# Another order of the attention part's steps in an explicit instruction sequence

## The chip, the cores and the metric

The kernel runs on one core of a Trainium2 chip. The metric is the device time of one execution in microseconds (us); three runs of the kernel before gave a median of 977.19 us (974.65 to 978.02). The engines are named as in the profile: PE (matrix products), DVE (vector), ACT (scalar functions), POOL (the second elementwise engine) and SP, which here only issues transfers.

## The reference

Three layers follow one another: sparse attention, and two feed-forward layers with different gates. 4 batches of 8 heads, 576 rows, 64 columns per head; the attention's output is 2304 rows of 512.

```python
scores = scale * np.matmul(q, k.transpose(0, 1, 3, 2))
thresh = np.max(scores, axis=-1, keepdims=True) - tau
scores = np.where(scores >= thresh, scores, -1000000000.0)
attn = np.exp(scores - np.max(scores, axis=-1, keepdims=True))
attn = attn / (np.sum(attn, axis=-1, keepdims=True) + 1e-09)
x = np.matmul(attn, v)                # then (B, H, S, D) -> (B*S, H*D)
h = x @ w_in                          # 512 -> 2048
g = h * np.tanh(np.log1p(np.exp(h)))
y = g @ w_out                         # 2048 -> 512
h = y @ w_in2
out = (h * np.clip(h + 3.0, 0.0, 6.0) / 6.0) @ w_out2
```

## The kernel before, in words

**Numbers.** Products of the feed-forward layers are made from pairs of f16 parts (a high part and a low rest) with three matmuls for each product. The weights come as 64-bit words and are converted on the chip, in eight groups for each matrix: `lr` loads a group of 1 MB (line 759), `zw` takes its maximum on DVE (line 681), `zd`, `zp`, `zt`, `zf` make a scale from it (ACT, PE, DVE, DVE), `c0_g_` scales on ACT (line 800), `c0_g_0` and `c0_g_1` shift on POOL (line 807), `c0_g_l` joins in the low words on DVE (line 820), `h` writes the high part on ACT (line 840), and `u` the low part on POOL (through line 627). Two buffers hold raw groups; group g+2 can be loaded when `c0_g_l` is done with group g.

**Attention.** Pairs of heads (n = 0 to 15, four to a batch) are worked through in query tiles c = 0 to 3 of 128 rows and a last one, c = 4, that holds 64 rows of both heads. The steps of a tile, for heads j = 0 and 1: `s` scores on PE (line 1697), `pk` the peak on DVE (line 1706), `ex` the exponential on ACT (line 1716), `th` the threshold on ACT (line 1711), `mk` the mask on DVE (line 1719), `ph` the high part on ACT (line 1724), `pl` the low part on POOL (line 627), `tr` a transpose done by a transfer on SP (line 1732), `pv` the product with v on PE (line 1745). Then `dt`, `dr`, `dn` normalise two tiles on DVE, `fl` transposes them on PE, and `xh` and `xl` write the two parts of x. There are two banks for scores (one head in each), so a score waits for the mask of the tile before; four buffers each for exponentials and for f16 parts; three for transposed tiles (`PV_DEEP`). The values of a batch need `lv` loads, `vm` maxima on DVE (line 1592), a common scale (`ve`, `zdv`, `zpv`, `ztv`, `vq`), and `vh` and `vl`, the two parts. `lk`, `lq` load k and q, `kh` scales k on ACT, `qp` pads q on POOL.

**First layer.** When all four pairs of a batch have x for 256 rows (a block), `g{fp}{j}_{i}_0_{blk}` are its products with `w_in` on PE (line 1112): 96 steps of two matmuls to a block, feature groups fp = 0 to 7 in order, each wanting its weight group. `t` takes the result out, `hs` stores it to memory, and it is read again for the gate when the attention is over. Of the nine blocks six are worked on during the attention in steps of two matmuls; PE does them between the steps of attention.

**Order.** Nothing is chosen at run time. `SEQUENCE` (line 62) lists all 4098 steps as name@engine, and `Plan.run` (line 565) issues them in that order. Each engine executes its own steps strictly in this order, SP its transfers too; between engines only data and buffers make one wait for another. A buffer goes to the next step that asks for it in the sequence, from those given back before, so the order also settles which buffer a step has to wait for.

Of the kernel before, what the change touches and what calls it, by code (L numbers as in the profile page):

```python
# [67 lines left out]
s1_0_0@pe vh1@act vl0@dve ph0_1_0@act s1_0_1@pe vl1@dve ph0_1_1@act pk1_0_0@dve vh2@act pl0_1_0@pool pk1_0_1@dve
ex1_0_0@act zw0_0@dve th1_0_0@act ex1_0_1@act kh0_3@act mk1_0_0@dve vh3@act mk1_0_1@dve s1_1_0@pe tr0_1_0@sp
ph1_0_0@act vl2@dve zd0_0@act s1_1_1@pe ph1_0_1@act pk1_1_0@dve pl1_0_0@pool pv0_0_0@pe pk1_1_1@dve ex1_1_0@act  # L70
zw0_1@dve th1_1_0@act ex1_1_1@act lv0_1@sp lv1_1@sp zp0_0@pe mk1_1_0@dve lv2_1@sp tr1_0_0@sp mk1_1_1@dve ph1_1_0@act
s2_0_0@pe zt0_0@dve ph1_1_1@act zf0_0@dve s2_0_1@pe zd0_1@act pl1_1_0@pool pk2_0_0@dve c0_0_@act pv0_1_0@pe
pk2_0_1@dve ex2_0_0@act vm1_1@dve th2_0_0@act zp0_1@pe ex2_0_1@act c0_0_1@pool mk2_0_0@dve tr1_1_0@sp mk2_0_1@dve
c0_0_0@pool ph2_0_0@act s2_1_0@pe zt0_1@dve ph2_0_1@act dt0_0@dve s2_1_1@pe dr0_0@dve pl2_0_0@pool zf0_1@dve dn0_0@dve
zx0_0_0@act pk2_1_0@dve c0_1_@act fl0_0@pe pk2_1_1@dve pv1_0_0@pe ex2_1_0@act tr2_0_0@sp c0_1_1@pool vm2_1@dve
th2_1_0@act ex2_1_1@act mk2_1_0@dve c0_1_0@pool pv1_1_0@pe xh0_0@act mk2_1_1@dve ph2_1_0@act c0_0_l@dve ph2_1_1@act
s3_0_0@pe s3_0_1@pe lr0_2@sp h0_0_@act xl0_0@dve u0_0_1@pool pk3_0_0@dve dt1_0@dve u0_0_0@pool ex3_0_0@act pk3_0_1@dve
dr1_0@dve th3_0_0@act vm0_1@dve ex3_0_1@act pl2_1_0@pool mk3_0_0@dve mk3_0_1@dve ph3_0_0@act s3_1_0@pe zw0_2@dve
ph3_0_1@act s3_1_1@pe tr2_1_0@sp pl3_0_0@pool dn1_0@dve pk3_1_0@dve fl1_0@pe zd0_2@act pv2_0_0@pe pk3_1_1@dve
ex3_1_0@act th3_1_0@act c0_1_l@dve ex3_1_1@act tr3_0_0@sp xh1_0@act mk3_1_0@dve h0_1_@act mk3_1_1@dve s0_2_0@pe  # L80
ph3_1_0@act u0_1_1@pool xl1_0@dve ph3_1_1@act s0_2_1@pe vl3@dve lr0_3@sp zp0_2@pe pk0_2_0@dve u0_1_0@pool lv3_1@sp
pv2_1_0@pe zt0_2@dve ex0_2_0@act pk0_2_1@dve pl3_1_0@pool zf0_2@dve th0_2_0@act ex0_2_1@act mk0_2_0@dve c0_2_@act
# [15 lines left out]
pk2_2_1@dve pv1_2_0@pe xh0_4@act xs0_4@sp pl1_4_0@pool th2_2_0@act zpv1_1@pe g11_6_0_0@pe zw0_5@dve ex2_2_1@act
tr1_3_0@sp g11_8_0_0@pe g11_10_0_0@pe g20_0_0_0@pe t1_0_0@act g20_2_0_0@pe qp5@pool g20_4_0_0@pe g20_6_0_0@pe
kh0_5@act g20_8_0_0@pe g20_10_0_0@pe g21_0_0_0@pe g21_2_0_0@pe g21_4_0_0@pe g21_6_0_0@pe c0_4_l@dve zd0_5@act  # L100
g21_8_0_0@pe g21_10_0_0@pe g30_0_0_0@pe tr1_4_0@sp t2_0_0@act g30_2_0_0@pe g30_4_0_0@pe mk2_2_1@dve g30_6_0_0@pe
h0_4_@act g30_8_0_0@pe g30_10_0_0@pe g31_0_0_0@pe mk2_2_0@dve s2_3_0@pe ph2_2_1@act u0_4_0@pool ztv1_1@dve lr0_6@sp
# [1916 lines left out]
```

## Time and profile before

| | |
|---|---|
| median of three runs | 977.19 us (974.65 to 978.02) |
| profiled execution | 974.99 us, span of its instructions 973.2 us |
| PE busy | 923.1 us, 95% of the span |
| DVE busy | 767.7 us, 79% |
| ACT busy | 649.9 us, 67% |
| POOL busy | 401.6 us, 41% |
| granted PE clock, mean | 0.975 |
| transfers | 164.47 MB, 169 GB/s over the span |

The profile's second part cuts the span into 40 slices: PE stands at 3, 6, 7, 9, 6 and 8 tenths in the first six and at 9 (90% or more) from there to the next to last slice; the DMA engines stand at 9 or 8 in the first 18 slices and fall behind them. The attention ends near 400 us. A row of a timeline gives start and duration of an instruction, engine, line, operation, what it writes and reads, and in brackets how long its engine had stood idle and what ended that. The waits are sums by engine and line over a stretch.

### The profile page before, as it was taken

The numbers are of one execution on the slowest core, as the hardware profiler recorded it, in microseconds if no ns is written. First come the engines' busy times: TensorE is split into PE (matmuls) and PEld (weight loads), VectorE is DVE, ScalarE is ACT, GpSimd is POOL, SyncE is SP. The second block draws the span as 40 slices with busy tenths as digits, with TensorE's granted clock in tenths as the row PEclk, the third lists the DMA queues.
The fourth block names the chain that finished last, engine by engine and source line by source line (L and its number), as shares of the span: only waits on it lengthen the run. The fifth ranks groups of instructions, "written<-read, shape, count | busy, mean of one in ns | idle before, by whom it ended". The sixth has DMA issues, their size and how long they took to land.

```text
span 973.2 us, 25802 instructions
## 1 busy us (share of the span) xinstructions
PE 923.1 (95%) x10776; PEld 798.0 (82%) x10776; DVE 767.7 (79%) x1432; ACT 649.9 (67%) x1051; POOL 401.6 (41%) x354
## 2 busy tenths in 40 slices
...
GB/s 320 192 240 225 245 220 216 243 252 204 252 227 260 230 215 242 232 242 177 232 229 177 287 178 303 246 212 20 61 27 37 61 24 39 62 23 40 24 1 45
DMA packets 201798, 164.47 MB, mean 169 GB/s; under 512 B 174161, under 2 KB 174929, under 8 KB 195281
## 3 DMA queue, kind: packets, MB, share of 16 engines
...
q10 hardware_dynamic: 240, 0.20, 0.1%
...
HBM read 84.28 MB, written 36.04 MB: 124 GB/s over the span
## 4 chain that ended last, share of the span: by engine, by line
PE 84%; DVE 7%; POOL 3%; DMA 3%; issue 2%; ACT 1%; SPq 0%; DVEq 0%; POOLq 0%; ACTq 0%
PE h_g L1112 17%; PE y_y L1226 17%; PE s_s L1697 8%; PE aux_pv L1745 6%; PE hp_g1a L1299 5%; PE h_g0a L1299 5%; PE hp_g1d L1299 2%; PE h_g0d L1299 2%; POOL p_ph L627 2%; PE h_g1b L1299 1%; PE hp_g0b L1299 1%; DMA pt_tr<-p_ph 1%; PE y_y___1_6_0_13898 L1449 1%; PE y_y___1_0_0_10254 L1449 1%; PE y_y___1_4_0_12684 L1449 1%
## 5 line engine op out<-in xcount | busy, mean ns | idle before, releaser
L627 POOL TENSOR_TENSOR p_ph<-e_ex,p_ph 128x128 f16<-128x128 f32 (+3 forms) x160 | 185.8, 1184 | 110.6 <-issue 54.9
L1449 PEld LDWEIGHTS <-gs_oh 128*128 128x128 f16 x1512 | 146.8, 98 | 16.6
L1299 PEld LDWEIGHTS <-w__h 128*128 128x128 f16 x2016 | 156.0, 98 | 0.6
L1706 DVE TENSOR_REDUCE nm_pk<-s_s 128x1 f32<-128x576 f32 x144 | 104.7, 751 | 31.1 <-PE s_s L1697 30.0
L1719 DVE SCALAR_TENSOR_TENSOR e_ex<-s_s,thr_th,e_ex 128x576 f32<-128x576 f32 x144 | 111.8, 811 | 18.2 <-ACT thr_th L1711 13.6
L1716 ACT ACTIVATE e_ex<-s_s,nm_pk 128x576 f32<-128x576 f32 x144 | 104.2, 730 | 17.8 <-DVE nm_pk L1706 14.8
L1697 PE MATMUL s_s<-kd_lk,qs_qp 64*128 64x288 f32 x440 | 80.7, 481 | 35.7 <-DVE e_ex L1719 26.8
L1724 ACT ACTIVATE p_ph<-e_ex 128x576 f16<-128x576 f32 x144 | 94.7, 679 | 11.5 <-DVE e_ex L1719 8.8
L1299 PEld LDWEIGHTS <-w__u 128*128 128x128 f16 x1008 | 98.6, 98 | 0.0
L1745 PEld LDWEIGHTS <-pt_tr 128*128 128x128 f16 x2016 | 81.6, 103 | 10.8 <-issue 6.9
L1697 PEld LDWEIGHTS s_s<-kd_lk,qs_qp 64*128 64x128 f32 x440 | 41.3, 204 | 56.9 <-issue 39.8
L1745 PE MATMUL aux_pv<-vh,pt_tr 128*128 128x65 f16 (+1 forms) x1296 | 86.8, 203 | 1.0 <-DMA pt_tr<-p_ph 1.0
L627 DVE TENSOR_TENSOR gs_oh<-g_ab,gs_oh 128x896 f16<-128x896 f32 x72 | 74.6, 1086 | 14.9 <-ACT gs_oh L1399 14.9
L1399 ACT ACTIVATE gs_oh<-g_ab 128x1792 f16<-128x1792 f32 x36 | 59.6, 1690 | 27.2 <-DVE g_ab L627 27.2
L1745 PE MATMUL aux_pv<-vl_vl,pt_tr 128*128 128x64 f16 x720 | 71.0, 203 | 0.0
L1383 ACT ACTIVATE g_ab<-g_ab,aux,hscales 128x512 f32<-128x512 f32 x72 | 54.1, 805 | 17.1 <-DVE g_ab L1327 17.1
L1160 ACT ACTIVATE he_t<-h_g,hin 128x512 f32<-128x512 f32 x63 | 42.9, 683 | 23.0 <-PE h_g L1112 19.0
L1197 ACT ACTIVATE hp_e<-hl_l 128x512 f32<-128x512 f32 x72 | 42.5, 596 | 21.7 <-DVE gs_gh L1206 21.3
L1389 DVE SCALAR_TENSOR_TENSOR g_ab<-g_ab,f 128x512 f32<-128x512 f32 x72 | 51.2, 746 | 5.0 <-ACT g_ab L1383 5.0
L1206 DVE SCALAR_TENSOR_TENSOR gs_gh<-hp_e,fscales,gs_gh 128x512 f16<-128x512 f32 x72 | 52.9, 742 | 2.1 <-ACT gs_gh L1200 2.0
L1200 ACT ACTIVATE gs_gh<-hp_e,fscales 128x512 f16<-128x512 f32 x72 | 47.4, 680 | 9.4 <-PE y_y L1226 8.8
L1317 ACT ACTIVATE s_ka<-h_g0a 128x512 f32<-128x512 f32 x27 | 16.1, 595 | 48.3 <-PE h_g0a L1299 48.2
...
## 6 DMA issues: line engine op xcount, KB each, us to landing
...
```

The source lines that it names most:

```text
L627: engine[e].tensor_tensor(dst, a, b, ALU.subtract)
L1112: mm(hv[:, j, :], wj[:, wl, c * P : (c + 1) * P], x.tile[:, c, xl, :], start=j == 0 and n == 0, stop=j == 1 and n == 11, skip_group_check= ...
L1226: mm(yv[:, h, :], wt[1][f // 2].tile[:, f % 2, wl, c * P : (c + 1) * P], gs[fp // COL].tile[:, fp % COL, gl, f % 2, :], start=fp == 0 and ...
L1299: mm(dst.tile[:, i * Q : (i + 1) * Q], wt[2][fp][wl].tile[:, right - 1, c * P : (c + 1) * P], x[xl].tile[:, c, left - 1], start=first and ...
L1399: nc.scalar.activation(part.tile[:, :, 0], g.tile[:, :, 1:], AF.Copy)
L1449: mm(region(p), part[:, gl, left - 1], wt[3][fp][wl].tile[:, right - 1], start=fp == n == 0 and spot(p)[1] == 0, stop=fp == NG - 1 and n == 2,
L1697: mm(s[j].tile[:, half, :HALF], lh[r], rh[r], start=m == 0, stop=m == len(terms) - 1,)
L1706: nc.vector.tensor_reduce(neg.tile[:, j : j + 1], sv(j), AX.XY, ALU.max, negate=True)
L1716: nc.scalar.activation(ev(j), sv(j), AF.Exp, bias=neg.tile[:, j : j + 1])
L1719: nc.vector.scalar_tensor_tensor(ev(j), sv(j), thr.tile[:, j : j + 1], ev(j), ALU.is_ge, ALU.mult)
L1724: nc.scalar.activation(p16.tile[:, j, :S], e_.tile[:, j], AF.Copy)
L1745: mm(ov[:, dst, :d], pt.tile[:, j, ch, :], part.tile[:, src, vc, :], start=i == j == ch == 0 and part is vh, stop=j == w - 1 and ch == 8, ...
```

## The change

Only `SEQUENCE` changes. Both versions hold the same 4098 steps, each on the same engine. Nearly every line of the attention part is another; from the second feed-forward layer on the steps of each engine stand in the same order (DVE's last 605, ACT's last 356, PE's last 321). The diff, cut to the lines of the opening that the text below speaks of:

```diff
 SEQUENCE = """
-qp0@pool lk0_0@sp qp1@pool qp2@pool qp3@pool lq0_0@sp lk1_0@sp lq1_0@sp lv0_0@sp lv1_0@sp lv2_0@sp kh0_0@act lv3_0@sp
-lk0_1@sp s0_0_0@pe kh1_0@act lq0_1@sp lk0_2@sp s0_0_1@pe lq0_2@sp pk0_0_0@dve lr0_0@sp vm0_0@dve ex0_0_0@act lr0_1@sp
-lk0_3@sp vm1_0@dve lq0_3@sp vm2_0@dve pk0_0_1@dve vm3_0@dve th0_0_0@act ex0_0_1@act mk0_0_0@dve kh0_1@act mk0_0_1@dve
...
-s2_4_0@pe dt1_2@dve ph2_3_1@act c0_5_0@pool vq1@dve tr2_2_0@sp s3_2_0@pe dr1_2@dve ph2_3_0@act pk2_4_0@dve
...
-zd0_6@act xh1_2@act hs3_0_0@sp pk3_2_0@dve s3_2_1@pe ph2_4_0@act lq0_6@sp tr2_3_0@sp ex3_2_0@act t4_0_0@act xl1_2@dve
-pl2_4_0@pool vh6@act dt1_4@dve pk3_2_1@dve zp0_6@pe kh0_6@act qp6@pool zt0_6@dve c0_5_l@dve th3_2_0@act ex3_2_1@act
-zf0_6@dve h0_5_@act mk3_2_0@dve c0_6_@act u0_5_0@pool zi0@dve lr0_7@sp s3_3_0@pe tr2_4_0@sp ph3_2_0@act u0_5_1@pool
-g50_0_0_0@pe c0_6_0@pool g50_2_0_0@pe mk3_2_1@dve g50_4_0_0@pe c0_6_1@pool g50_6_0_0@pe dr1_4@dve pk3_3_0@dve
-s3_3_1@pe dn1_4@act ph3_2_1@act ex3_3_0@act g50_8_0_0@pe pk3_3_1@dve pl3_2_0@pool g50_10_0_0@pe g51_0_0_0@pe
-g51_2_0_0@pe zw0_7@dve th3_3_0@act g51_4_0_0@pe ex3_3_1@act g51_6_0_0@pe fl1_4@pe pv2_2_0@pe xh1_4@act mk3_3_0@dve
...
-zt0_7@dve fl2_2@pe mk3_4_0@dve pv2_4_0@pe pl3_3_0@pool xh2_2@act zf0_7@dve ph3_4_0@act s4_0_1@pe t5_0_0@act
...
-th4_1_0@act ex4_1_1@act mk4_1_0@dve xs2_4@sp t6_0_0@act tr3_4_0@sp vh5@act s5_0_0@pe ph4_1_0@act zs0@dve pv3_3_0@pe
-tr4_0_0@sp c0_7_l@dve mk4_1_1@dve h0_7_@act vl4@dve s5_0_1@pe lr1_1@sp ph4_1_1@act dt3_2@dve u0_7_0@pool lv0_2@sp
...
+lv1_0@sp lk0_0@sp lv3_0@sp lk1_0@sp lq0_0@sp lq1_0@sp lv0_0@sp vm1_0@dve lv2_0@sp lr0_0@sp lk0_1@sp kh0_0@act lq0_1@sp
+lr0_1@sp kh1_0@act s0_0_0@pe s0_0_1@pe pk0_0_0@dve vm3_0@dve ex0_0_0@act pk0_0_1@dve vm2_0@dve th0_0_0@act ex0_0_1@act
+mk0_0_0@dve mk0_0_1@dve ph0_0_0@act s0_1_0@pe vm0_0@dve ph0_0_1@act s0_1_1@pe ve0@dve pl0_0_0@pool pk0_1_0@dve
...
+ex2_3_1@act zpv1_1@pe zw0_5@dve pl2_2_0@pool g21_4_0_0@pe pv1_3_0@pe ex2_3_0@act th2_3_0@act ztv1_1@dve g21_6_0_0@pe
...
+pk3_2_0@dve t3_0_0@act ph2_4_0@act pk3_2_1@dve zd0_6@act c0_5_l@dve ex3_2_1@act zp0_6@pe g40_0_0_0@pe pl2_4_0@pool
+pv1_4_0@pe ex3_2_0@act g40_2_0_0@pe th3_2_0@act zt0_6@dve g40_4_0_0@pe h0_5_@act lr0_7@sp vq1@dve g40_6_0_0@pe
+g40_8_0_0@pe hs3_0_0@sp zf0_6@dve g40_10_0_0@pe mk3_2_0@dve c0_6_@act u0_5_1@pool tr2_4_0@sp mk3_2_1@dve s3_3_0@pe
+ph3_2_0@act c0_6_0@pool dt1_4@dve dr1_4@dve pk3_3_0@dve g41_0_0_0@pe kh0_6@act g41_2_0_0@pe g41_4_0_0@pe g41_6_0_0@pe
+c0_6_1@pool ex3_3_0@act g41_8_0_0@pe g41_10_0_0@pe zx0_0_2@act s3_3_1@pe ph3_2_1@act u0_5_0@pool pk3_3_1@dve
+pl3_2_0@pool g50_0_0_0@pe th3_3_0@act g50_2_0_0@pe tr2_3_0@sp dn1_4@act mk3_3_0@dve g50_4_0_0@pe fl1_4@pe g50_6_0_0@pe
+zw0_7@dve xh1_4@act g50_8_0_0@pe ph3_3_0@act s3_4_0@pe ex3_3_1@act c0_6_l@dve zd0_7@act lq0_5@sp g50_10_0_0@pe vh4@act
...
+dr2_2@dve s4_0_1@pe zi0@dve pk4_0_1@dve pv2_4_0@pe dn2_2@dve th4_0_0@act c0_7_0@pool g60_0_0_0@pe ph3_4_0@act
...
+ex4_1_1@act g61_10_0_0@pe pv3_3_0@pe xh2_4@act ex4_1_0@act u0_7_0@pool mk4_1_1@dve xs2_4@sp tr4_0_0@sp kh0_5@act
+mk4_1_0@dve ph4_1_1@act vl4@dve s5_0_0@pe t5_0_0@act s5_0_1@pe dt3_2@dve ph4_1_0@act pk5_0_0@dve g70_0_0_0@pe
...
```

On SP alone, the transfers from the weight group 5 to the first of `w_out` read, before: `lr0_5 lk0_5 lq0_5 xs0_4 tr1_3_0 tr1_4_0 lr0_6 hs1_0_0 tr2_2_0 lk0_6 hs3_0_0 lq0_6 tr2_3_0 lr0_7 tr2_4_0 xs1_4 tr3_2_0 lk0_7 lq0_7 lr1_0`; now: `lr0_5 tr1_3_0 lr0_6 xs0_4 tr1_4_0 hs1_0_0 tr2_2_0 lq0_6 lk0_6 lr0_7 hs3_0_0 tr2_4_0 tr2_3_0 lq0_5 lr1_0`. The pads `qp0` to `qp3`, ahead of everything on POOL before, now stand behind `pl0_0_0`, `c0_1_1`, `c0_4_1` and `pl1_4_0`. The maxima `vm1_1`, `vm2_1`, `vm3_1`, on DVE behind `pk2_0_1`, `pk2_1_1` and `pk0_3_1` before, stand behind `mk0_2_1`, `pk0_4_0` and `mk1_2_1`.

## Rows read from the trace of the kernel before

**Rows 1.** Busy us (instructions) by engine, granted clock, DMA share, GB/s, by windows.
```profile
core 0: us, PE busy (x) PEld busy (x) DVE busy (x) ACT busy (x) POOL busy (x), PEclk, DMA share, GB/s
0.00:150.00 150.00, 106.99 (x1036) 75.65 (x1037) 121.18 (x244) 111.05 (x194) 96.12 (x104) 0.84 0.98 239
...
0.00:25.00 25.00, 9.93 (x38) 5.08 (x39) 17.88 (x35) 16.48 (x28) 7.18 (x22) 1.00 0.95 317
50.00:75.00 25.00, 18.37 (x197) 13.16 (x196) 21.99 (x47) 18.37 (x33) 20.42 (x19) 0.73 0.97 234
...
100.00:125.00 25.00, 18.86 (x177) 13.05 (x177) 14.54 (x36) 15.98 (x30) 15.09 (x15) 0.73 1.05 253
...
425.00:450.00 25.00, 25.00 (x233) 22.44 (x231) 21.12 (x32) 20.55 (x34) 9.31 (x6) 1.00 0.53 197
```

**Rows 2.** Waits of PE from 0 to 150 us: sum, times, longest.
```profile
PE s_s L1697 <- DVE e_ex L1719: 26.8, 10, 4.6
```

**Rows 3.** Waits of PE from 150 us to the end.
```profile
PE aux_fl L1824 <- DVE xn_dn L1787: 0.8, 1, 0.8
PE aux_pv L1745 <- DMA pt_tr<-p_ph: 0.5, 1, 0.5
```

**Rows 4.** Groups of instructions over the span: busy, mean ns, idle before.
```profile
L1706 DVE TENSOR_REDUCE nm_pk<-s_s 128x1 f32<-128x576 f32 x144 | 104.7, 751 | 31.1 <-PE s_s L1697 30.0
L1719 DVE SCALAR_TENSOR_TENSOR e_ex<-s_s,thr_th,e_ex 128x576 f32<-128x576 f32 x144 | 111.8, 811 | 18.2 <-ACT thr_th L1711 13.6
```

**Rows 5.** Timeline of the start: first score, v maxima, second peak, first masks.
```profile
5.14 2.71 PE L1697 MATMUL s_s<-kd_lk,qs_qp 64*128 64x288 f32 x8 [5.14 <-DMA qs_qp<-in_q]
...
8.32 1.74 DVE L1592 TENSOR_REDUCE vt_vm<-v_lv 128x1 f32<-128x640 f32 x2 [0.20 <-DMA v_lv<-in_v]
9.97 0.75 DVE L1706 TENSOR_REDUCE nm_pk<-s_s 128x1 f32<-128x576 f32 x1
...
11.37 1.53 DVE L1719 SCALAR_TENSOR_TENSOR e_ex<-s_s,thr_th,e_ex 128x576 f32<-128x576 f32 x2
```

**Rows 6.** Waits of DVE from 0 to 150 us.
```profile
DVE nm_pk L1706 <- PE s_s L1697: 14.0, 16, 2.6
DVE top L681 <- DMA raw_lr<-in_moe_w_in: 5.2, 3, 3.2
```

**Rows 7.** Timeline of DVE: the last low part of block 0's x.
```profile
71.37 0.41 DVE L627 TENSOR_TENSOR x_fl<-aux_fl,x_fl 128x256 f16<-128x256 f32 x1
```

**Rows 8.** Timelines of SP, POOL and DVE from 99 to 113 us.
```profile
99.27 6.13 SPq L1732 DMA_TRANSPOSE pt_tr<-p_ph  x1
105.50 0.52 SPq L759 DMA_DIRECT2D raw_lr<-in_moe_w_in  x1
...
103.68 2.27 POOL L627 TENSOR_TENSOR w__h__1_1373<-cvt_c__1_1258,w__h__1_1373 128x512 f16<-128x512 f32 x2 [4.34 <-ACT w__h__1_1373 L840]
...
107.67 0.76 DVE L1706 TENSOR_REDUCE nm_pk<-s_s 128x1 f32<-128x576 f32 x1 [2.60 <-PE s_s L1697]
111.65 1.22 DVE L681 TENSOR_REDUCE top<-raw_lr 128x1 f32<-128x1024 f32 x1 [3.22 <-DMA raw_lr<-in_moe_w_in]
```

**Rows 9.** Timelines of POOL, DVE and PE: last weight group; pair 5's first tiles.
```profile
132.53 2.48 POOL L627 TENSOR_TENSOR w__h__1_1732<-cvt_c__1_1597,w__h__1_1732 128x512 f16<-128x512 f32 x2 [3.92 <-ACT w__h__1_1732 L840]
...
132.86 0.75 DVE L1706 TENSOR_REDUCE nm_pk<-s_s 128x1 f32<-128x576 f32 x1
...
136.88 2.03 PE L1697 MATMUL s_s<-kd_lk,qs_lq 64*128 64x288 f32 x8
```

**Rows 10.** Line 820 (last step of a weight's conversion): duration ns min/median/max, first and last start.
```profile
L820 DVE SCALAR_TENSOR_TENSOR cvt_c__1_371<-raw_lr,cvt_c__1_371 x1: 1661/1661/1661, 37.6 to 37.6; 128x1024 uint32<-128x1024 uint32 x1
...
L820 DVE SCALAR_TENSOR_TENSOR cvt_c__1_824<-raw_lr,cvt_c__1_824 x1: 2016/2016/2016, 73.9 to 73.9; 128x1024 uint32<-128x1024 uint32 x1
L820 DVE SCALAR_TENSOR_TENSOR cvt_c__1_954<-raw_lr,cvt_c__1_954 x1: 1216/1216/1216, 84.4 to 84.4; 128x1024 uint32<-128x1024 uint32 x1
```

**Rows 11.** Waits of SP from 0 to 150 us.
```profile
SPq L1732 <- POOL p_ph L627: 33.2, 9, 7.9
```

**Rows 12.** Waits of SP from 150 to 400 us.
```profile
SPq L1732 <- PE aux_pv L1745: 4.7, 3, 2.3
```

More of the change, by code (lines that the diff above doesn't have):

```diff
@@ L68 @@
[L68 to L82, printed above, removed]
@@ L98 @@
[L98 to L102, printed above, removed]
@@ L123 @@
-th4_1_0@act ex4_1_1@act mk4_1_0@dve xs2_4@sp t6_0_0@act tr3_4_0@sp vh5@act s5_0_0@pe ph4_1_0@act zs0@dve pv3_3_0@pe
-tr4_0_0@sp c0_7_l@dve mk4_1_1@dve h0_7_@act vl4@dve s5_0_1@pe lr1_1@sp ph4_1_1@act dt3_2@dve u0_7_0@pool lv0_2@sp
-pk5_0_0@dve dr3_2@dve ex5_0_0@act pk5_0_1@dve u0_7_1@pool g70_0_0_0@pe dn3_2@dve th5_0_0@act g70_2_0_0@pe ex5_0_1@act
-mk5_0_0@dve pl4_1_0@pool fl3_2@pe pv3_4_0@pe xh3_2@act mk5_0_1@dve ph5_0_0@act xl3_2@dve ph5_0_1@act zf1_0@dve
-s5_1_0@pe dt3_4@dve vh7@act vl5@dve s5_1_1@pe tr4_1_0@sp g70_4_0_0@pe c1_0_@act dr3_4@dve pl5_0_0@pool g70_6_0_0@pe
@@ new lines @@
+zx0_0_1@act g20_10_0_0@pe mk2_2_1@dve zdv1_1@act g21_0_0_0@pe g21_2_0_0@pe h0_4_@act s2_3_1@pe xl0_2@dve qp3@pool
+s2_3_0@pe xh0_4@act pk2_3_1@dve ph2_2_0@act u0_4_0@pool xs0_4@sp pv1_2_0@pe tr1_4_0@sp ph2_2_1@act pk2_3_0@dve
+ex2_3_1@act zpv1_1@pe zw0_5@dve pl2_2_0@pool g21_4_0_0@pe pv1_3_0@pe ex2_3_0@act th2_3_0@act ztv1_1@dve g21_6_0_0@pe
+t1_0_0@act dt1_2@dve g21_8_0_0@pe mk2_3_0@dve g21_10_0_0@pe zd0_5@act hs1_0_0@sp t2_0_0@act dr1_2@dve zp0_5@pe
+s2_4_0@pe u0_3_1@pool zt0_5@dve tr2_2_0@sp zf0_5@dve mk2_3_1@dve g30_0_0_0@pe u0_4_1@pool c0_5_@act g30_2_0_0@pe
@@ new lines @@
+pk2_4_0@dve g30_4_0_0@pe g30_6_0_0@pe g30_8_0_0@pe zw0_6@dve g30_10_0_0@pe ph2_3_1@act s3_2_0@pe c0_5_0@pool
+ex2_4_0@act lq0_6@sp dn1_2@dve g31_0_0_0@pe lk0_6@sp th2_4_0@act c0_5_1@pool g31_2_0_0@pe ph2_3_0@act fl1_2@pe
+mk2_4_0@dve g31_4_0_0@pe g31_6_0_0@pe xh1_2@act g31_8_0_0@pe pl2_3_0@pool xl1_2@dve g31_10_0_0@pe s3_2_1@pe
+pk3_2_0@dve t3_0_0@act ph2_4_0@act pk3_2_1@dve zd0_6@act c0_5_l@dve ex3_2_1@act zp0_6@pe g40_0_0_0@pe pl2_4_0@pool
+pv1_4_0@pe ex3_2_0@act g40_2_0_0@pe th3_2_0@act zt0_6@dve g40_4_0_0@pe h0_5_@act lr0_7@sp vq1@dve g40_6_0_0@pe
@@ new lines @@
+mk4_0_1@dve xh2_2@act vh5@act tr3_3_0@sp pl3_4_0@pool dn2_4@dve s4_1_1@pe ph4_0_0@act s4_1_0@pe xl2_2@dve c0_7_l@dve
+ph4_0_1@act g60_8_0_0@pe g60_10_0_0@pe pl4_0_0@pool fl2_4@pe g61_0_0_0@pe tr3_4_0@sp pk4_1_1@dve g61_2_0_0@pe
+h0_7_@act g61_4_0_0@pe g61_6_0_0@pe pk4_1_0@dve g61_8_0_0@pe pv3_2_0@pe lk0_7@sp zw1_0@dve th4_1_0@act lr1_1@sp
+ex4_1_1@act g61_10_0_0@pe pv3_3_0@pe xh2_4@act ex4_1_0@act u0_7_0@pool mk4_1_1@dve xs2_4@sp tr4_0_0@sp kh0_5@act
+mk4_1_0@dve ph4_1_1@act vl4@dve s5_0_0@pe t5_0_0@act s5_0_1@pe dt3_2@dve ph4_1_0@act pk5_0_0@dve g70_0_0_0@pe
@@ new lines @@
+pk5_0_1@dve g70_2_0_0@pe pl4_1_0@pool ex5_0_0@act g70_4_0_0@pe g70_6_0_0@pe dr3_2@dve g70_8_0_0@pe dn3_2@dve
+th5_0_0@act g70_10_0_0@pe ex5_0_1@act mk5_0_0@dve fl3_2@pe pv3_4_0@pe mk5_0_1@dve ph5_0_0@act s5_1_0@pe t6_0_0@act
+u0_7_1@pool tr4_1_0@sp s5_1_1@pe xh3_2@act pk5_1_0@dve ph5_0_1@act pk5_1_1@dve g71_0_0_0@pe ex5_1_0@act g71_2_0_0@pe
+pl5_0_0@pool g71_4_0_0@pe xl3_2@dve g71_6_0_0@pe th5_1_0@act g71_8_0_0@pe ex5_1_1@act dt3_4@dve g71_10_0_0@pe
+mk5_1_0@dve g00_0_0_1@pe hs5_0_0@sp g00_2_0_1@pe vh6@act lq0_7@sp g00_4_0_1@pe mk5_1_1@dve g00_6_0_1@pe g00_8_0_1@pe
@@ new lines @@
+g21_10_0_1@pe g30_0_0_1@pe tr6_1_0@sp mk7_0_0@dve g30_2_0_1@pe ph7_0_1@act g30_4_0_1@pe g30_6_0_1@pe g30_8_0_1@pe
+c1_1_@act zs0@dve g30_10_0_1@pe g31_0_0_1@pe s7_1_1@pe s7_1_0@pe ph7_0_0@act t2_0_1@act lv2_2@sp pk7_1_0@dve
+pl7_0_0@pool pv5_1_0@pe pk7_1_1@dve ex7_1_0@act g31_2_0_1@pe g31_4_0_1@pe dt5_0@dve dr5_0@dve g31_6_0_1@pe th7_1_0@act
+dn5_0@dve g31_8_0_1@pe ex7_1_1@act mk7_1_0@dve g31_10_0_1@pe pv6_0_0@pe t3_0_1@act qp7@pool mk7_1_1@dve tr7_0_0@sp
+s4_2_0@pe vl7@dve ph7_1_1@act s4_2_1@pe ph7_1_0@act pk4_2_0@dve g40_0_0_1@pe g40_2_0_1@pe pk4_2_1@dve pl7_1_0@pool
```

776 lines of the change are left out of this document (389 added, 387 removed).

## The prediction

> **What bounds the kernel now.** I read the busy time by windows first. TensorE (PE) is busy 107.0 of the first 150 us, at a mean granted clock of 0.84, and without a break in the windows behind; from 425 to 450 us its 233 matmuls of 256 columns leave 107 ns each, and nothing is left between them [rows 1]. The waits of PE say the same from the other side: behind 150 us the longest single wait in 820 us is 0.8 us [rows 3], while in the first 150 us PE stands 26.8 us, in ten waits, before score matmuls (`s`) because DVE has not masked the scores that occupy the bank (`mk`, line 1719) [rows 2]. So all work behind the opening is a queue in front of a full PE, and its length does not depend on order. The time can change by what PE loses in the opening (43.0 us idle, and the stretches at half clock: the granted clock is 0.73 of full from 50 to 75 and from 100 to 125, a mix of the levels 2.4 and 1.2 GHz [rows 1]), and by new holes that the new order tears later.
>
> Inside the opening the reader should see a loop. Two banks hold scores; a score matmul waits for the mask of the tile before, the mask for the peak (`pk`) and the exponential. One tile needs two peaks of 0.75 us and two masks of 0.81 us on DVE [rows 4], and DVE takes everything in its written order: the v maxima (`vm`), the weight maxima (`zw`), the last step of a weight's conversion (`c..l`). From 50 to 75 us DVE is 88% busy; from 100 to 125 only 58% [rows 1]. There it waits itself: 14.0 us of the opening for scores from PE, 5.2 us for weight loads (`lr`) [rows 6]. The two wait for each other, and order decides how long.
>
> **The change part by part.** No step is added, removed or put on another engine; 4098 steps stand in another order. I count on each engine's own order, set it against the durations in the rows, and let a step begin when its engine is free and what it needs is there. From pair 4 on both orders have nearly the same filler at the same place (before `s5_0_0` 84 first-layer steps `g` in both, before `s8_2_0` 335 and 333, before `s12_0_0` 429 and 431), so what counts lies before it. The sum is the lead of the attention chain at `s5_1_0`, where PE has nearly equal work behind it (86 and 90 `g`).
>
> *The first loads.* SP now asks for `lv1`, `lk0`, `lv3`, `lk1` ahead of the first half of q, where only `lk0` was. Two v tiles of 320 KB and 144 KB of k more, at the 317 GB/s of the first window [rows 1], are 2.5 us: the first score moves from 5.1 to 7.6 us. DVE loses less. It had to do three v maxima between the first two peaks, began the second at 9.97 and the first mask at 11.37 [rows 5]. Now one maximum runs before the first peak, and one each after the two peaks: the first mask at 12.1 us. Lag 0.7 us. Two tiles on it is 1.3, and at the second tile of pair 1 it is 2.5, of which 0.9 is scale arithmetic of the first weight group done ahead. Two of the three waits for weight loads (5.2 less 3.2, that is 2.0 us [rows 6, 8]) then take it up, since those loads come as early as before and DVE comes later. At 52 us: +0.8. Bounds: 0 to +2.5.
>
> *52 to 74 us.* Three v maxima of batch 1 (0.81 each, the row of two takes 1.74 [rows 5]) have moved into this stretch, two from far ahead. DVE has no slack to hide them: +1.7. The last low part of block 0's x, at 71.4 us before [rows 7], ends 2.5 us later, and with it the first `g`. Bounds: +0.8 to +3.
>
> *74 to 100 us.* Before, 43 `g` stood ahead of `s2_3_0` and 53 ahead of `s2_4_0` and `s3_2_0`; now 32, 36 and 42. A `g` step of two matmuls is 0.22 us, so scores come up to 3.7 us earlier, and DVE's waits for PE (14.0 in all [rows 6]; about 3.6 of them here) go. `zw0_5` moves behind `pk2_3`. -2.5, no lag at `c0_5_l` (near 100 us). The `g` moved back fill waits behind it. Bounds: 0 to -3.6.
>
> *100 to 115 us.* Before, the load of the last weight group (`lr0_7`) was queued behind a transpose whose issue held SP 6.13 us, left at 105.5, and DVE stood 3.22 us at its maximum, 111.65, with masks and peaks behind it [rows 8]. Now `lr0_7` stands ahead of `tr2_4` and `tr2_3`, asks at about 100.6, as soon as `c0_5_l` gives its buffer free, and lands before DVE gets to `zw0_7`. Next to that, `s3_3_1` stood behind `g` steps of feature group 5, whose weights POOL ended at 106 us, and DVE waited 2.60 us for it [rows 8]; now only steps of group 4 stand ahead of it. I count PE at full clock here; at half, as in much of this window before, each score costs 0.6 us more. What is late next is ACT: `ex3_2_0` stands behind `t3_0_0`, which wants twelve `g`, about 1 us. Queued behind `lr0_7` on SP are `hs3_0_0` and both transposes; their `pv` stand behind `s3_3`. -3.2 for the load, -0.8 net for the score: -4. Bounds: 0 to -5.8.
>
> *115 to 137 us.* `s4_0_1` stood behind `pv2_4_0`, now ahead of it; `zs0` no longer stands before `c0_7_l`. So the last weight group is converted earlier (POOL at 132.5 before [rows 9]; I get about 124), and `pk5_0_0`, 132.9 before [rows 9], comes at 127. -2. Against it: ACT takes `kh0_5` right ahead of `s5_0_0`, 0.8 us, which is in this. Bounds: +1 to -4.
>
> Lead at `s5_1_0` (136.9 before [rows 9]): 0.8 + 1.7 - 2.5 - 4 - 2 = -6.0. Given back: block 1's x is complete at about 133, so PE waits once more, +1. Behind that I allow +0.5 for small holes in the full stretch. Sum: **-4.5 us**.
>
> *What hides the rest.* The pads (`qp`), moved behind the first `pl` on POOL, write columns first read by the fifth tile of a pair: nothing. `pv` and `fl` stand later, behind more `g`, in most tiles: nothing while a transpose buffer is free (third rival).
>
> *A shared resource.* Of the eight `c..l` of the opening three took 1.66 to 2.02 us, with POOL at work beside them, and five 1.22 [rows 10]. Which will meet POOL in the new order I cannot tell: bounds -2.4 (the three no longer do, 0.80 each at most) and +4.0 (the five do as well); I take 0, the row nearest to no change.
> The Trainium skill (SBUF — State Buffer, section "SBUF: two separate sides") has VectorE instructions with two SBUF inputs and GpSimd hold one port pair in turn. The trace agrees, by that 0.80; by the rule the sum has the same two ends.
>
> The profiled run before took 974.99 us (span 973.2), 2.2 under the median of the runs, 977.19. So 970.5 on the scale of the profile, **972.7** on that of the median.
>
> **The rivals.**
> 1. *The transfer queue paces the opening; nothing changes.* For it: the DMA engines' share is 0.97 and 1.05 in windows of the opening [rows 1], the transposes' issue holds SP up to 6 us at a time [rows 8], and all transfers are the same. Against it: SP waits 33.2 us of the opening for POOL alone before transposes [rows 11], so the queue is often empty-handed. If right, later landings take the lead back as it arises: 977.
> The Trainium skill (Perfetto Trace Analysis, section: What "DMA-bound" means) counts an issuing engine whose track is solid with DMA slices as a bound of its own. By it this rival would hold; SP's 33.2 us of waiting speak against.
> 2. *The late start is carried on; slower.* Place: DVE at 74 us, lag 2.5. If the maxima are dearer than I see, or the lag reaches c0_5_l so that `lr0_7` leaves no earlier than 103, the 3.2 us wait stays in part while the lag stays whole. For it: DVE 88% busy there [rows 1]. Price: +2.5 + 1 = +3.5, 980.7. It decides once less than 2.5 of the 6 us are won back behind 74.
> 3. *The later `pv` fill the ring of three transposed tiles.* SP then stands at a transpose until `pv` has run, and PE later at the next `pv`. For it: SP already waited 4.7 us, in three waits up to 2.3, for that between 150 and 400 us [rows 12]. Against it: PE felt none of them over 0.5 [rows 3]. Four such waits that reach PE cost 9.2, which turns -4.5 into +4.7: 981.9.
>
> **How the numbers follow.** A measurement can tell about 0.3%, 2.9 us, from no change. Forecast 0.57: its own range, 967 to 974, is faster. Rival 1: 0.18, the same. Rival 2: 0.17 and rival 3: 0.08, slower. So faster 0.57, same 0.18, slower 0.25. The range reaches from 966.5 (all good bounds of the 100 to 137 us stretch, with the start's lag) to 981, which takes in rival 2.
>
> **What would show it.** Right: the first score at about 7.6 us; DVE's wait for `raw_lr` at the last weight group gone, its maximum near 108; POOL done with the last weight before 130; the peak of `s5_0_0` near 127; PE idle about 38 to 39 us in the first 150, and a granted clock above 0.73 from 100 to 125. Wrong: the masks of pair 3 no earlier than before, or PE waits behind 150 us over 3 us in sum.

## The result, and the profile after

The changed kernel takes 980.75 us, the median of 20 runs (975.29 to 986.05), against 975.0 (20 runs, 972.67 to 981.46) of the kernel before on the same chip: 1.0052 of its time, with a 95% interval of 1.0035 to 1.0069. By that ratio it is 5.1 us slower; I had forecast 4.5 us faster. The profiled execution took 980.68 us, span 978.9.

Busy time by windows, after (columns as in [rows 1]):

```profile
0.00:150.00 150.00, 106.98 (x1064) 74.26 (x1064) 124.50 (x241) 111.51 (x198) 97.72 (x101) 0.87 0.98 238
...
100.00:125.00 25.00, 18.35 (x191) 12.48 (x192) 21.84 (x44) 19.68 (x37) 20.49 (x19) 0.98 1.05 258
150.00:211.00 61.00, 59.32 (x743) 46.89 (x743) 50.95 (x99) 50.19 (x93) 40.92 (x41) 1.00 1.11 237
211.00:400.00 189.00, 184.16 (x2220) 145.16 (x2218) 150.63 (x271) 149.19 (x284) 114.91 (x108) 1.00 1.05 225
```

The two windows behind the opening in the kernel before, which [rows 1] do not have:

```profile
150.00:211.00 61.00, 60.51 (x746) 47.83 (x746) 51.80 (x95) 53.06 (x98) 40.47 (x38) 1.00 1.04 236
211.00:400.00 189.00, 188.09 (x2315) 148.81 (x2312) 152.57 (x279) 153.30 (x287) 118.26 (x110) 1.00 1.07 230
```

Read PE's idle time off them (window less PE busy). In the first 150 us it is 43.0 in both kernels, but after has done 1064 matmuls by then, before 1036, at a granted clock of 0.87 against 0.84. From 150 to 211 it grows from 0.5 to 1.7, from 211 to 400 from 0.9 to 4.8. So the opening is a little ahead, and what was full before is not full now.

Waits of PE from 150 us to the end, after; [rows 3] are its counterpart:

```profile
PE aux_pv L1745 <- DMA pt_tr<-p_ph: 3.5, 4, 1.4
PE y_y L1226 <- DVE gs_gh L1206: 1.4, 1, 1.4
PE s_s L1697 <- DVE den_dt L1783: 1.0, 1, 1.0
PE s_s L1697 <- DVE e_ex L1719: 0.8, 3, 0.4
PE h_g L1112 <- DVE he_t L1162: 0.5, 1, 0.5
PE h_zpy L657 <- ACT dgb_zdy L652: 0.4, 1, 0.4
PE h_zp L657 <- ACT dgb_zd L652: 0.4, 1, 0.4
```

They are 8.5 us with two small ones that are left out here, 2.0 before. The largest was 0.5 before: PE reaches `pv` before the transposed tile (`tr`) has landed. `y`, `h` and the two scale products lie behind 403 us, where I had foreseen nothing at all.

The opening by its marks, after: first score, load of the last weight group, its maximum, the peak of `s5_0_0`, POOL's last weight step (against [rows 5, 8, 9]):

```profile
9.32 2.29 PE L1697 MATMUL s_s<-kd_lk,qs_lq 64*128 64x288 f32 x8 [9.32 <-DMA qs_lq<-in_q]
...
104.34 0.33 SPq L759 DMA_DIRECT2D raw_lr<-in_moe_w_in  x1
...
110.95 1.21 DVE L681 TENSOR_REDUCE top<-raw_lr 128x1 f32<-128x1024 f32 x1
...
131.45 1.42 DVE L1706 TENSOR_REDUCE nm_pk<-s_s 128x1 f32<-128x576 f32 x2
...
134.76 1.16 POOL L627 TENSOR_TENSOR w__h__1_1627<-cvt_c__1_1537,w__h__1_1627 128x512 f16<-128x512 f32 x1
```

One profile is one execution, and the opening differs between them. 13 profiled kernels, after and twelve of the experiments, share the changed opening, and five the old one. Where PE starts the scores of some tiles (us):

| | changed opening, median (from, to) | old opening, median | gain, forecast |
|---|---|---|---|
| first score | 8.0 (7.5 to 9.3) | 5.1 | -2.9, -2.5 |
| `s0_2_0` | 50.5 (49.4 to 53.6) | 49.8 | -0.7, -0.8 |
| `s1_3_0` | 73.7 (71.3 to 76.2) | 70.5 | -3.2, -2.5 |
| `s4_0_0` | 112.2 (109.7 to 114.7) | 115.6 | 3.4, 4.0 |
| `s5_1_0` | 132.5 (130.4 to 134.8) | 136.8 | 4.3, 6.0 |

The profile of after, 9.3 to 134.6, is at the late end of all of them.

### The profile page after: what moved, and what is told of

It reads as the page before. It is cut to its first block, busy times and chain, and to the rows that moved or that the text cites. A ratio compares the mean times of both kernels' runs of the same rounds, so it can differ in the third digit from the quotient of the medians.

```text
span 978.9 us, 25757 instructions
## 1 busy us (share of the span) xinstructions
PE 921.8 (94%) x10776; PEld 795.0 (81%) x10776; DVE 765.9 (78%) x1432; ACT 646.0 (66%) x1051; POOL 400.6 (41%) x354
## 3 DMA queue, kind: packets, MB, share of 16 engines
q8 instruction: 85, 1.39, 0.6%
## 4 chain that ended last, share of the span: by engine, by line
PE 61%; DVE 17%; ACT 6%; DMA 4%; issue 2%; POOL 0%; DVEq 0%; SPq 0%; ACTq 0%
PE y_y L1226 11%; PE h_g L1112 9%; PE h_g0a L1299 5%; PE hp_g1a L1299 5%; PE s_s L1697 4%; DVE e_ex L1719 3%; PE aux_pv L1745 3%; DVE nm_pk L1706 3%; PE hp_g1d L1299 2%; PE h_g0d L1299 2%; ACT e_ex L1716 2%; DMA pt_tr<-p_ph 2%; DVE gs_gh L1206 2%; PE h_g1b L1299 1%; PE hp_g0b L1299 1%
## 5 line engine op out<-in xcount | busy, mean ns | idle before, releaser
L1697 PE MATMUL s_s<-kd_lk,qs_lq 64*128 64x288 f32 x600 | 108.7, 476 | 33.1 <-DVE e_ex L1719 15.1
L1706 DVE TENSOR_REDUCE nm_pk<-s_s 128x1 f32<-128x576 f32 x144 | 104.6, 751 | 27.5 <-PE s_s L1697 26.4
L1697 PEld LDWEIGHTS s_s<-kd_lk,qs_lq 64*128 64x128 f32 x600 | 55.8, 203 | 63.7 <-issue 45.8
```

The costliest lines, as they stand in the source:

```text
L1697: mm(s[j].tile[:, half, :HALF], lh[r], rh[r], start=m == 0, stop=m == len(terms) - 1,)
L1706: nc.vector.tensor_reduce(neg.tile[:, j : j + 1], sv(j), AX.XY, ALU.max, negate=True)
```

## The experiments

CHANGED and BEFORE stand for the two lists of steps; a sum of parts means that the later part leaves out what the earlier has done. A ratio is to the kernel before, run on the same chip.

**Opening or rest?** Four cuts.

```diff
-SEQUENCE = CHANGED
+e1_open:  CHANGED[:740] + BEFORE
+e2_rest:  BEFORE[:750] + CHANGED
+e3_start: BEFORE[:187] + CHANGED
+e4_tail:  CHANGED[:2360] + BEFORE
```

> The changed order up to its 740th step (about 150 us), then what is left of the steps in the order before. Theory A (the new order behind 150 us tears its own holes): the lead of 3.9 us that the changed kernel shows at s7_1_0 is kept, 971.1 against 975.0 before, and PE waits under 2.5 us behind 150 us. Theory B (the opening leaves the transfers behind, 1.4 MB fewer in the first 25 us, so that later transposes land late whatever the order): the lead is lost again as in the changed kernel, 977 to 980, with PE waits for transposed tiles of 3 us or more between 150 and 400.

981.94 us, 1.0061 (1.0040 to 1.0083). Neither theory: the cut tore a hole of its own. DVE's order had a v maximum right behind the cut whose load SP had not yet asked for. PE's and DVE's longest waits from 150 to 403 us in e1_open:

```profile
PE s_s L1697 <- DVE e_ex L1719: 7.6, 1, 7.6
...
DVE vt_vm L1592 <- DMA v_lv<-in_v: 4.6, 1, 4.6
```

> The order before up to its 750th step (about 150 us), then what is left of the steps in the changed order. Theory A: the holes come although the opening is the old one, 975.0 + 7 to 9 = 982 to 984, with PE waits of 5 us or more behind 150 us. Theory B: with the transfers not behind, the holes stay away, 975 to 976.

981.42, 1.0062 (1.0043 to 1.0080). As theory A has it, but 6.0 us, not 7 to 9: with the old opening the new order behind 150 us costs about as much as the whole change does (the two intervals overlap).

> The order before up to its 187th step (about 48 us: first loads, first tiles of pairs 0 to 3), then the changed order. The changed kernel is 5.5 us late at s3_0_0. Theory A: these 5.5 us come back whole, 980.75 - 5.5 = 975.3, and the holes behind 150 us stay (PE waits there 6 to 9 us). Theory B: the start comes back and the holes shrink with it, 971 to 973. A third reading (the late start is caught up by the waits for weight loads before 100 us, as I forecast): within 1.5 us of the changed kernel, 979.3 to 980.75.

980.79, 1.0053 (1.0035 to 1.0071): the third reading. The late first score costs nothing at the end; it is caught up before 100 us.

> The changed order up to its 2360th step (the end of the attention, about 403 us), then the order before. Between 403 us and the end the changed kernel loses about 2.2 us more to PE waits than the one before (y for gs 1.4, h and two scale products). Theory A: these go, 978.5. If they come only from engines that are late at the end of the attention: 980 to 981.

978.27, 1.0030 (1.0012 to 1.0049). Theory A: of the 5.1 us, the order behind 403 us accounts for 2.1 by the two ratios.

**Cuts meant to leave no hole, and single causes.**

```diff
-SEQUENCE = CHANGED
+e5_blend:    each step between its two places, from 148 to 190 us; then BEFORE
+e7_from_220: CHANGED[:1290] + BEFORE
+e9_v3:       CHANGED, with vm3_3 behind dr9_4, ve3 and zdv3_3 behind pk11_2_1 on DVE
```

e8_no_stores is this edit of the changed kernel, e10_before_no_stores the same edit of the one before:

```diff
-                    nc.sync.dma_start(out=hd[blk][:, fp // 2], in_=he.tile)
+                    if blk not in (2, 3, 4):
+                        nc.sync.dma_start(out=hd[blk][:, fp // 2], in_=he.tile)
...
-                    at = hd[blk][:, fp // 2 : fp // 2 + COL // 2]
+                    at = hd[1 if blk in (2, 3, 4) else blk][:, fp // 2 : fp // 2 + COL // 2]
```

> The changed order up to 148 us, then step by step over into the order before, which holds alone from about 190 us on (each step's place is a mean of its two places, with a weight that goes from the one to the other), so that no seam is left like the one of e1_open, where PE stood 7.6 us behind a v maximum whose load came late. Theory A (order behind 150 us makes the holes): the lead of 3.2 to 3.9 us at 150 is kept to the end, 975.5 - 3.5 = 972.0, PE waits behind 150 under 2 us. Theory B (transposed tiles land no earlier for a PE that is early, so a lead at 150 is given back): waits for transposed tiles of 2 us or more between 200 and 300, 974.5 to 976.

980.84, 1.0069 (1.0045 to 1.0093). Inconclusive: the mixture has holes of 6.5 us before scores between 150 and 200.

> The changed order up to its 1290th step (about 220 us), then what is left in the order before. Against e4_tail (978.3), which has the changed order to 403 us: theory A takes away the loss of 2.6 us at 275 to 300 that every kernel with the changed order there shows, and about 1 us behind it: 974.7. Theory B: the holes before pv8_3 and pv9_2 (1.0 and 1.1 us in e4_tail) come back in the old order too, because the lead is there: 976.5 to 977.

978.39, 1.0035 (1.0018 to 1.0052). Inconclusive for the same reason: a v maximum behind the cut waited 5.3 us for its load, and PE 4.1 us behind it.

> The changed kernel, which leaves out the stores of h of blocks 2 to 4 (hs, 12 of 512 KB each, between 160 and 330 us); their readers take block 1's. Theory B (the transposed tiles are late because SP's transfers are a full queue): PE's waits for transposed tiles behind 150 us fall from 3.5 to under 1 us, and the time to 977.5. Theory A: these waits hardly change, 980 to 981.

977.41, 1.0010 (0.9992 to 1.0028): theory B's number. PE's waits for transposed tiles fell to one of 1.7 us, before 211 us. The profile is that of the fastest of the twelve runs. The control, e10, stands below.

> The changed kernel with three steps of DVE moved: the maximum, the binade and the diagonal of the values of batch 3 (vm3_3, ve3, zdv3_3), which take 2.5 us ahead of the peak pk10_4_0 at 285 us, stand behind mk10_4_0 and pk11_2_1, as before. If they make the hole before s11_2_1 and its neighbours: the loss at 275 to 300 falls by 2 us and the time to 978.7. If DVE is late there in any case, 980 to 981.

980.86, 1.0057 (1.0036 to 1.0077). The 1.0 us wait of PE for `den_dt` is gone from its profile, and nothing is won in the time. PE's waits for transposed tiles at 278 and 287 us (1.1 and 0.9 us) are still there, as in after at 273 and 282 (1.4 and 0.7).

**Controls and parts.**

```diff
-SEQUENCE = CHANGED
+e12_open2:      e1_open, with vm0_2 behind mk7_0_1
+e13_sp_order:   e4_tail, with SP's steps from 740 to 1950 in the order of BEFORE
+e14_tail_alone: BEFORE[:2357] + CHANGED
```

> The kernel before, which leaves out the same stores of h of blocks 2 to 4 as e8_no_stores (readers take block 1's). It is the control: the changed kernel came down by 3.3 us without them. Theory B (only a PE that is early meets transposed tiles that are late): PE before waits 0.5 us for transposed tiles behind 150, so at most 1 us is to be had, 974.5 to 975.7. If fewer transfers help any order (through the readers, or the DMA engines in general): as much as in the changed kernel, 972.

972.72, 0.9974 (0.9962 to 0.9986). The kernel before gains too, 0.26%, where the changed one gained 0.42% (1.0052 to 1.0010). So most of e8's gain is not special to the changed order. About 0.16% is left, 1.6 us, which the three intervals (0.12 to 0.18% to either side each) do not tell from nothing.

> As e1_open, the changed order up to 150 us and then the one before, with the v maximum that made the seam (vm0_2) moved behind mk7_0_1, some 10 us later. Theory A, in which order alone decides: the 7.6 us wait at the seam goes and the lead of 3.2 is kept: 972 to 973. Theory B: waits for transposed tiles come up as PE is early, 975 to 976. A third reading (the old order behind the new opening is no better than the new one): 979 or more.

977.62, 1.0037 (1.0025 to 1.0049). Still a hole at the cut (4.3 us in one wait of PE for a mask, behind the next v maximum): inconclusive, but 2.3 us better than e1_open by the two ratios.

> As e4_tail (978.3: the changed order to 403 us, the order before from there), but SP's transfers alone stand in the order before from 150 to about 320 us. Now k, q and v of the next pairs are asked for in other places among the transposes (before tr8_2_0 three loads now, one store before). If SP's order makes the transposed tiles late: PE's waits for them fall from 3.5 to about 1 us and the time to 975 to 976. If it is the lead of PE, whatever the order on SP: 978 to 979, waits as in e4_tail.

995.52, 1.0211 (1.0196 to 1.0226). Neither: PE waits 7.4 us in one go for a mask and 8.1 in all for tiles. So putting back SP's order by itself tears other holes; that the other engines' orders fit SP's is my reading, not a measurement.

> The order before up to its 2357th step (403 us) and the changed order from there. The reverse of e4_tail: if the changed order of the last first-layer and the first second-layer products costs 2.2 to 2.5 us by itself, 975.6 + 2.3 = 977.9, with a wait of y for gs of 1.4 to 2 us. If it only costs behind a late attention: 975.6.

978.2, 1.0028 (1.0014 to 1.0042): theory A, 2.7 us. Its profile, of the fastest of the twelve runs, has the same four waits of PE behind 403 us as after, 1.7 us in sum where before has 0.5:

```profile
PE h_g L1112 <- DVE he_t L1162: 0.5, 1, 0.5
PE y_y L1226 <- DVE gs_gh L1206: 0.4, 1, 0.4
PE h_zpy L657 <- ACT dgb_zdy L652: 0.4, 1, 0.4
PE h_zp L657 <- ACT dgb_zd L652: 0.4, 1, 0.4
```

The kept traces say the same without the opening's spread. From the last score of the attention (`s15_4_0`) to the end, the seven kernels with the new order there take 589.9 to 592.3 us, and the thirteen with the old one 587.7 to 588.6.

**The stretch from 211 us, the ring of tiles, and one step of the sum alone.**

```diff
-SEQUENCE = CHANGED
+e15_seam211:       CHANGED[:1157] + BEFORE
+e16_pv_later:      e15_seam211, with pv6_3_0 behind g41_10_0_2, dt6_2 behind mk7_3_1
+e18_stretch_alone: BEFORE[:1161] + CHANGED[:2360] + BEFORE
+e19_no_debt:       e16_pv_later, with vl8 behind mk8_0_1, vl9 behind t6_0_2
```

e17_four_tiles is the changed kernel with

```diff
-PV_DEEP = 3
+PV_DEEP = 4
```

> The changed order up to its 1157th step (about 211 us, the first score of pair 8), then the order before; no v step is under way at the seam. Theory A (the new order behind 211 loses the lead): the lead of 3.2 us less the hole of 1.4 us before pv6_3_0 is kept: 973. Theory B (transposed tiles land no earlier for an early PE): PE waits for transposed tiles of 2 us or more between 211 and 320, 975 to 976. A new 4 us wait at the seam would leave it open again.

977.2, 1.0016 (1.0001 to 1.0031), and in its profile PE waits 3.8 us for tiles and 1.7 before `fl6_2`. Between the theories.

> As e15_seam211, with pv6_3_0 six steps of g later on PE (1.3 us) and dt6_2, which reads it, behind mk7_3_1 on DVE. In the changed kernel PE stood 1.3 us before pv6_3_0 for its transposed tile, which landed at 207.2 us. Theory A: that hole goes, 1 us below e15_seam211: 972. Theory B: the wait comes back at the next transposed tile, no difference.

975.54, 1.0010 (0.9989 to 1.0030). The wait before `pv6_3_0` fell from 2.1 to 1.0; one of 2.8 at the cut is in its place.

> The changed kernel with four transposed tiles instead of three. My third rival (later pv fill the ring of three): SP's wait for pv of 4.4 us goes, PE's waits for transposed tiles fall from 3.5 to about 1 us, 977 to 978. If the ring has no part in it: 980 to 981.

982.27, 1.0061 (1.0039 to 1.0083): the ring has no part in it. SP's wait for `pv` is gone, and nothing is won. PE's waits from 150 to 403 us with four tiles:

```profile
PE aux_pv L1745 <- DMA pt_tr<-p_ph: 5.6, 6, 2.1
```

> The order before up to its 1161st step (about 213 us), the changed order to the end of the attention (403 us), the order before behind that. Both kernels with the changed stretch and only one other part changed gave 0.30% (with the opening) and 0.62% (with the end, 0.28% by itself). Theory A: the stretch costs 3.3 us by itself, 978.5. Theory B: without the lead it costs little, 975 to 976.

978.54, 1.0033 (1.0016 to 1.0049): theory A. The order from 211 to 403 us costs 3.2 us on its own, with no lead in front of it. Its window has the same hole as after, 5.1 us of PE idle:

```profile
211.00:400.00 189.00, 183.91 (x2228) 144.26 (x2227) 150.25 (x274) 149.44 (x284) 114.27 (x107) 1.00 1.05 222
```

> As e16_pv_later (975.5), with the two low parts of v that DVE made at the seam (vl8, vl9, 3.6 us together there) behind mk8_0_1 and pk8_1_0. There PE stood 2.8 us before fl6_2, which waits for dn6_2 behind them. Theory A: that wait goes and the lead lasts: 972.5 to 973.5, below both kernels. Theory B: waits for transposed tiles between 215 and 300 take it: 975 to 976.

975.0, 0.9992 (0.9976 to 1.0007): theory B's number, and its sign is there too. The wait before `fl6_2` is gone. PE reaches `s8_0_0` at 207.7 us, where kernels with the old order up to there have 209.9 to 213.7, and then, in the old order, waits 2.1 us for transposed tiles between 215 and 300 us. The longest of these waits:

```profile
221.03 0.20 PE L1745 MATMUL aux_pv<-vh,pt_tr 128*128 128x65 f16 x1 [1.32 <-DMA pt_tr<-p_ph]
```

By the ratio the new order to 211 us, with its two holes mended, is worth 0.8 us, and the interval holds no change.

e20_load_alone is the kernel before with these steps moved and no others:

```diff
-lq0_6@sp tr2_3_0@sp ... lr0_7@sp ... tr2_4_0@sp
+lq0_6@sp ... lr0_7@sp tr2_3_0@sp ... tr2_4_0@sp
-pv2_2_0@pe pv2_3_0@pe s3_4_0@pe s4_0_0@pe
+pv2_2_0@pe s3_4_0@pe pv2_3_0@pe s4_0_0@pe
-mk3_3_1@dve dt2_2@dve pk3_4_0@dve dr2_2@dve pk4_0_0@dve
+mk3_3_1@dve pk3_4_0@dve pk4_0_0@dve dt2_2@dve dr2_2@dve
```

> The order before, with the load of the last weight group (lr0_7) ahead of the transpose tr2_3_0 on SP; to let it, the product pv2_3_0 stands behind s3_4_0 on PE and dt2_2 and dr2_2 behind pk4_0_0 on DVE. My prediction gave 3.2 us for this step: DVE's wait of 3.2 us at the last weight group goes, and the end comes 3 us earlier, 972.5. If a lead won in the opening is given back later, or its waits only move to the next transposed tile: 975 to 976, with PE's idle time up to 150 us no less than 42.

972.62 us, 0.9971 (0.9957 to 0.9984) of the kernel before: faster than both kernels, by 2.8 us where I had put 3.2. The load now goes out before the transpose, and DVE waits 0.32 us for it where it stood 3.22 [rows 8]. Timeline of e20_load_alone (its lines are numbered one higher):

```profile
100.50 0.34 SPq L760 DMA_DIRECT2D raw_lr<-in_moe_w_in  x1
100.93 9.19 SPq L1733 DMA_TRANSPOSE pt_tr<-p_ph  x2
...
108.77 1.22 DVE L682 TENSOR_REDUCE top<-raw_lr 128x1 f32<-128x1024 f32 x1 [0.32 <-DMA raw_lr<-in_moe_w_in]
```

The lead lasts: all of PE's waits from 150 us to the end in e20_load_alone are

```profile
PE aux_pv L1746 <- DMA pt_tr<-p_ph: 0.9, 2, 0.5
PE aux_fl L1825 <- DVE xn_dn L1788: 0.8, 1, 0.8
PE h_g L1113 <- DVE he_t L1163: 0.3, 1, 0.3
PE aux_fl L1831 <- ACT xtail L1800: 0.2, 1, 0.2
```

so an early PE need not meet late tiles in the old order: here `s8_0_0` starts at 209.7 us. In e19_no_debt it starts at 207.7, and there the tiles are late. How much lead the old order can keep is open between these two.

## Why the prediction was wrong

**The step that failed.** It is "Behind that I allow +0.5 for small holes in the full stretch", with the premise that "all work behind the opening is a queue in front of a full PE, and its length does not depend on order". The order from 211 to 403 us costs 3.2 us by itself (e18_stretch_alone) and the order behind 403 us 2.7 (e14_tail_alone). Together these are 5.9 where I had 0.5, and e2_rest shows 6.0; each has an interval of 1.4 to 1.8 us to either side, so that they meet so closely is in part luck. I compared the two orders up to pair 4, saw the same filler at the same place behind it, and counted only `g` steps there. In the old order the tiles of this stretch came just in time, as the rows below show for one of them, and that is a property of the order too. Why the end costs 2.7 is open: only 1.2 us more of PE's waits show there in e14_tail_alone.

**What waits in the stretch.** Low part of a tile on POOL, its transpose on SP, and SP's transfers between them, at `tr8_2_0`, before:

```profile
256.31 2.74 POOL L627 TENSOR_TENSOR p_ph<-e_ex,p_ph 128x128 f16<-128x128 f32 x2 [1.41 <-issue]
...
254.93 3.42 SPq L1732 DMA_TRANSPOSE pt_tr<-p_ph  x1
258.39 0.57 SPq L1168 DMA_DIRECT2D hd<-he_t  x1
259.14 3.37 SPq L1732 DMA_TRANSPOSE pt_tr<-p_ph  x1
```

and after:

```profile
254.16 2.53 POOL L627 TENSOR_TENSOR p_ph<-e_ex,p_ph 128x128 f16<-128x128 f32 x2 [1.46 <-issue]
...
255.44 3.34 SPq L1732 DMA_TRANSPOSE pt_tr<-p_ph  x1
258.89 0.52 SPq L1168 DMA_DIRECT2D hd<-he_t  x1
259.52 0.37 SPq L1609 DMA_DIRECT2D v_lv<-in_v  x1
259.94 0.95 SPq L1848 DMA_DIRECT2D td<-xts_fl  x1
261.06 3.79 SPq L1732 DMA_TRANSPOSE pt_tr<-p_ph  x1
```

Before, the low part ends at 259.05 and its transpose starts at 259.14. After, the low part is 2.4 us earlier, at 256.69, and the transpose starts at 261.06, 4.4 us behind it: the transpose of another pair, a store, a load of v and a store of x stand in front on SP. (Between that other transpose and `tr8_2_0` these are two stores and a load, not the three loads that the expectation of e13_sp_order names; before, it was the one store.) The next three tiles of two heads (`tr8_3_0`, `tr9_2_0`, `tr9_3_0`) wait 2.3, 2.7 and 4.1 us in the same way, and PE waits 1.39 us for `tr8_3_0`:

```profile
273.17 0.20 PE L1745 MATMUL aux_pv<-vh,pt_tr 128*128 128x65 f16 x1 [1.39 <-DMA pt_tr<-p_ph]
```

These gaps go with the order of the stretch, whatever the opening. In the seven kernels that have the new one there with all stores (after, e2, e3, e4, e9, e17, e18) the four are 4.0 to 5.1, 1.5 to 3.2, 1.9 to 3.1 and 2.7 to 4.3 us; in the eight with the old one (before, e1, e5, e7, e12, e14, e15, e16) and in e19 and e20 none is over 1.1. From `s8_0_0` to `s15_4_0` PE takes 175.8 to 177.9 us in those seven, with 3.6 to 5.4 us of idle time, and 171.7 to 173.8 in before, e1, e5, e10, e12, e14 and e20, which have the old stretch and no cut in it, with 0.9 to 2.4 us.

That SP's queue makes the four transposes late is borne out by e8: in the new order without the twelve stores the gaps are 0.7 us and three times 0.03, no wait of PE for a tile over 0.2 us is left in the stretch, which takes 173.3 us with 1.6 us of idle time; in its control e10 these are 171.7 and 0.9. Leaving out the stores takes away both their places on SP and their bytes, and which of the two counts is open. How much of the 3.2 us hangs on these transposes stays open too. In the seven profiles PE's waits for transposed tiles are 0.9 to 3.1 us of the idle time in the stretch, and the rest stands before scores and `fl`, behind DVE and ACT. In times e8 against e10 gives 1.6 us, not clear of noise. With SP's old order alone (e13) the four gaps are at most 0.5, but the stretch takes 179.3 us by other holes.

The Trainium skill (Perfetto Trace Analysis, section: What "DMA-bound" means) calls a kernel bound by its issuing engine where that engine's track is solid with DMA slices. From 254 to 282 us SP's slices fill 26.1 of the 28 us before and 26.4 after, and from 211 to 400 us 87% before and 81% after, yet the order that is less full loses: here the rule does not tell the two apart.

**Point by point.** *First loads, +0.8 at 52 us*: right, 0.7 in the median; the first score came at 7.5 to 9.3 us, and e3_start shows that it costs nothing. *52 to 74, +1.7*: 2.5, within its bounds: 3.2 late at `s1_3_0` where I had 2.5. *74 to 115, -2.5 and -4*: right in sum, with a lead of 3.4 at `s4_0_0` where I had 4.0. DVE's wait for `raw_lr` is gone from its waits, the granted clock of 100 to 125 us rose from 0.73 to 0.98. In the profile of after alone, `lr0_7` left at 104.34, not 100.6, with `zw0_7` at 110.95, not 108; over the 13 kernels the medians are 101.0 and 109.0. *115 to 137, -2*: half, -0.9: POOL ended its last weight step at 135.9, not before 130, and the peak of `s5_0_0` came at 131.45, not 127. *What would show it*: PE idle 43.0 in the first 150, not 38 to 39; PE did more at a higher clock in the same idle time, which I had not taken for a possibility. In that profile PE's waits for masks in the opening fell from 26.8 to 14.3 us, but its waits for transposed tiles rose from 0.5 to 4.2, for the diagonals of the weight scales (`zd`) from nothing to 4.1, and the one for q from 5.1 to 9.3; I had put nothing for the tiles. "PE waits behind 150 us over 3 us in sum" was the sign of being wrong, and it is there, with 8.5. *The range*: its lower end does not come out of its terms, which give 977.2 - 5.8 - 4 + 1.5 = 968.9 with the stretches up to 100 us as forecast, not 966.5. That 980.75 lies inside it is luck: the upper end of 981 was set for rival 2, which did not happen.

**The lead that was won.** Nine kernels have the new order at least up to 211 us, in opening and stretch to there, and four have the old one. By their medians the new order leads by 5.2 us at `s7_1_0` and by 3.1 at `s8_0_0` (211 us), where it starts between 207.0 and 215.0 us against 209.9 to 213.7. In after and in e15 a hole before `pv6_3_0`, shortly ahead of `s8_0_0`, takes 1.3 and 2.1 of it. At the end little is left: the whole change, 5.1 us, less what the stretch and the end cost by themselves, 5.9, leaves the opening to 211 us a gain of 0.8; e19_no_debt says 0.8, too, and neither is clear of noise. Two places where the lead goes can be seen. In e19_no_debt it is waits for transposed tiles. In kernels with the new end it is the end itself: behind `s15_4_0` those with the old opening (e2, e14) take 589.9 us, with a wait of PE for `gs` of 0.4 to 0.5, and those with the new order from 48 us or earlier (after, e3, e8, e9, e17) 590.9 to 592.3, with one of 1.4 to 2.0 us.

**The rivals.** Rival 1 (the queue paces, nothing changes) had the right engine, SP, but in the opening, and not the sign. Rival 2 (the late start is carried on) is out by e3_start. Rival 3 named a wait that is there, PE before `pv` for a transposed tile, 3.5 us where it had 9.2; but its reason, a full ring of three tiles, is out by e17_four_tiles. So its 981.9, close to the measured 980.75, is luck. I gave it 0.08.
